# A broadcast maximum, the normaliser inside the memory matrix, and half-width stationary operands in the tail blocks of an attention and gated-MLP kernel

## The chip, the cores and the metric

The kernel runs on one core of one Trainium2 chip. The metric is the device time of one execution in microseconds (us); smaller is better. The engines are named as in the profile: PE (TensorE matmuls), PEld (its loads of stationary operands), DVE (VectorE), ACT (ScalarE), POOL (GpSimd) and SP (SyncE, which issues most DMAs).

## The reference

Attention over four batches of 576 rows and eight heads of width 64, with a gated read of a memory matrix, and then a gated MLP on all 2304 rows:

```python
scores = scale * np.matmul(q, k.transpose(0, 1, 3, 2))
scores = np.where(causal, -1000000000.0, scores)
scores = scores - scores.max(-1, keepdims=True)
a = np.exp(scores)
a /= a.sum(-1, keepdims=True) + 1e-09
local = np.matmul(a, v)
...
mem_ret = np.einsum('bhsd,bhde->bhse', q_p, M_prev)
mem_norm = np.einsum('bhsd,bhd->bhs', q_p, z_prev)[..., None] + 1e-06
mem_out = mem_ret / mem_norm
g = 1.0 / (1.0 + np.exp(-beta))[None, :, None, None]
return (g * mem_out + (1 - g) * local).astype(np.float32)
...
rms = np.sqrt(np.mean(x * x, axis=-1, keepdims=True) + 1e-06)
xn = x / rms * rms_g
g = xn @ w_gate
silu = g * (1.0 / (1.0 + np.exp(-g)))
val = xn @ w_val
return (silu * val @ w_out).astype(np.float32)
```

Here q_p is phi(q) = elu(q) + 1, and the MLP is 512 to 1536 to 512.

## The kernel before

The 2304 rows are 18 blocks of 128. Each batch has four full blocks and a rest of 64 rows; the rests of two batches share a block. These two shared blocks, 10 and 17, are called tail blocks. Blocks 0 to 3 are the first block of each batch and are computed in float32. All later blocks split each operand into a high and a low float16 part and add three products. Two blocks make a chunk of the MLP; a chunk has 12 slices F of gate and value projections (`m_proj`, tile gv) and 12 slices of the output projection (`m_down`, tile out).

The parts that matter here, with the letter under which `keep` records their instructions:

- Z, `over_partitions`: a maximum over the 128 partitions. A matmul with the column as stationary operand (L257) turns it into a row, DVE reduces the row (L259), and a second matmul (L260) spreads the result to all partitions; its reader takes it from PSUM. It is called for z, for the gain, for M of batches 0 and 1, for K and V of these batches (two columns each), for the three thirds of the gate and value weights (two columns each) and for the output weights.
- p and u, `pair_memory` and `mem32`: for blocks 0 to 3, M of a pair of heads stands in one block-diagonal tile (Mpair) and z in another (zpair). Four matmuls give the retrieved values (L786) and four give the normaliser (L790, two columns each).
- S, `u_scores` and `tail_scores`: in a tail block, the scores of one batch's rows stand in PSUM partitions 0 to 63 and those of the other in 64 to 127. Each matmul takes only half of the stationary columns (L632, L643).
- P, `u_pv` and `tail_pv`: P times V. In a tail block every head does it twice with all 128 stationary columns, once with each batch's V, into two PSUM tiles (L746 to L748); of each result only the half that belongs to that batch is read.
- M, `mem_mm`: reading the memory, in a tail block likewise twice at full width (L846).
- V, `loc_evac`: DVE scales the results out of PSUM (L877, L883).
- G is `m_proj`, D is `m_down`, U is `f64_to_f32` (a weight piece made float32 by two ACT instructions and one on DVE), E is the exponential, R turns the normalised rows of blocks 0 and 1.

The order on each engine is written out by hand: the table `ISSUE` holds a text for each engine, and `issue_in_order` reads it from left to right. `G4` takes the next four recorded instructions of kind G; `S~3` takes the one that stands fourth among those of kind S that are left. Every instruction is tied to the one before it, so each engine works strictly in that order and whatever waits holds all that stands behind it.

Of the kernel before, what the change touches and what calls it, by code (L numbers as in the profile page):

```python
# [17 lines left out]
ALU = mybir.AluOpType  # L18
AX = mybir.AxisListType
# [58 lines left out]
        "PSMPSS~3MPSS~2MPSS~1MPS2MPSMP15D6D~2G14D3S6DG9DD~2G5SGSGSGSGSGSGD2P24D3D~2GS6D4G13DD~2M8D4G4SGDD~2SGSGSGSGSG8D4"
        "G3MDD~2GMGMGMGMGMGD4GMGP25MPGPG3SGSGSGS3DD~2S3D4P9S3DD~2S4G24D4S4~2G6SGSG5P9G12S2D6G2P9G3SGSGSGSGSGSG14D6G5MGMGM"
        "GMGMP18GMGMGMG5SGSGSGSGSGSG2D6G5SGSGSGSGSGSP9G7SPGSPGSPGSPGSPGSPGPGP2D6G5MGMGMGMGMGMGMGMGP8GPG3SGSGSGSGSGSG2D6G5"  # L80
        "SGSGSGSGSGSG7P9G7D3SDSDSDGSGSGSP9GSGSG12SGSGSGSGSGSGSGSD6G5SGSGSGSGSP18GSGSGSG12D4MDMDMGMGMGP9MGMGMG12SGSGSGSGSG"
        "SGSGSD6G2P5GPGPGPSGPSGPSGPSGPSGSGSGSG5SGPSGPSGPSGPSGPSGPSGPSP5D6G9PGMPGMPGMPGMPGMPGMPGMPGMPGPGPGPGSGSGSGS5D6G9SG"
# [1457 lines left out]
```

## Time and profile before

| | |
|---|---|
| median of 3 runs | 624.98 us |
| lowest, highest | 621.99 us, 628.53 us |
| span of the profiled execution | 626.3 us |
| PE busy in it | 603.0 us, 96% |
| DVE, ACT, POOL busy | 438.0, 395.9, 134.6 us |
| first matmul | 6.0 us after the span's start |

The device time of the profiled execution is not listed apart; its span of 626.3 us lies within the three times, 1.3 us above their median. A busy share counts from an instruction's start to its modelled end, and matmuls overlap, so PE's 603.0 us are not work at its peak. What one matmul takes from its successor is read from the distance of their starts.

### The profile page before, as it was taken

The numbers are of one execution on the slowest core, as the hardware profiler recorded it, in microseconds if no ns is written. First come the engines' busy times: TensorE is split into PE (matmuls) and PEld (weight loads), VectorE is DVE, ScalarE is ACT, GpSimd is POOL, SyncE is SP. The second block draws the span as 40 slices with busy tenths as digits, with TensorE's granted clock in tenths as the row PEclk, the third lists the DMA queues.
The fourth block names the chain that finished last, engine by engine and source line by source line (L and its number), as shares of the span: only waits on it lengthen the run. The fifth ranks groups of instructions, "written<-read, shape, count | busy, mean of one in ns | idle before, by whom it ended". The sixth has DMA issues, their size and how long they took to land.

```text
span 626.3 us, 15885 instructions
## 1 busy us (share of the span) xinstructions
PE 603.0 (96%) x6124; PEld 474.2 (76%) x6124; DVE 438.0 (70%) x1287; ACT 395.9 (63%) x856; POOL 134.6 (21%) x221
## 2 busy tenths in 40 slices
PE   5979999999999999999999999999999999999996
PEld 4967887767876877888787877777788777887774
DVE  3557579989999796966777768697976756652221
ACT  4557669799789685777465656785875645523221
POOL 2040011105233222221221231122132212122111
PEclk9989999999999999999999999999999999999999
DMA  7969244588896978879388677749886544530001
GB/s 249 359 190 409 71 160 144 151 203 155 182 161 94 216 142 133 168 135 170 61 136 175 106 152 126 147 85 176 154 161 119 90 82 94 90 58 18 35 0 35
DMA packets 183787, 87.57 MB, mean 140 GB/s; under 512 B 165792, under 2 KB 165792, under 8 KB 183712
## 3 DMA queue, kind: packets, MB, share of 16 engines
q1 hardware_dynamic: 180640, 81.82, 60.9%
q10 hardware_dynamic: 3072, 4.74, 2.4%
q8 instruction: 48, 0.79, 0.6%
q14 instruction: 27, 0.22, 0.1%
HBM read 37.77 MB, written 4.72 MB: 68 GB/s over the span
## 4 chain that ended last, share of the span: by engine, by line
PE 68%; DVE 12%; DMA 7%; ACT 7%; issue 3%; SPq 1%; POOL 1%; DVEq 0%; ACTq 0%; POOLq 0%
PE gv L1108 28%; PE gv L1101 5%; PE out L1184 5%; PE out L1183 5%; PE out L1182 5%; DMA kv<-in_qkv_dram 4%; PE sc L609 3%; ACT junk L392 2%; PE tp L532 2%; DVE P L691 2%; PE sc L598 2%; DVE S L615 2%; DMA qT<-row 2%; DVE row L218 1%; PE csum L276 1%
## 5 line engine op out<-in xcount | busy, mean ns | idle before, releaser
L1108 PE MATMUL gv<-xT,wgv 128*128 128x256 f16 x2304 | 310.0, 273 | 0.5 <-DMA xT<-x 0.5
L1108 PEld LDWEIGHTS <-wgv 128*128 128x128 f16 x2304 | 220.0, 98 | 41.4 <-issue 2.4
L1147 POOL TENSOR_TENSOR h<-th,h 128x256 f16<-128x256 f32 x88 | 65.5, 744 | 282.2 <-ACT h L1146 275.3
L672 ACT ACTIVATE S<-S,nm 128x256 f32<-128x256 f32 (+3 forms) x112 | 70.7, 640 | 49.8 <-DVE nm L615 30.5
L691 DVE SCALAR_TENSOR_TENSOR P<-S,P 128x512 f16<-128x512 f32 (+2 forms) x96 | 67.7, 706 | 21.5 <-ACT P L189 21.0
L609 PE MATMUL sc<-kT,qT 128*128 128x128 f16 x576 | 79.3, 219 | 3.2 <-DVE nm L615 2.1
L1126 DVE SCALAR_TENSOR_TENSOR th<-th,gv 128x256 f32<-128x256 f32 x96 | 39.8, 415 | 60.4 <-ACT th L1125 60.1
L1125 ACT ACTIVATE th<-gv,wt 128x256 f32<-128x256 f32 x96 | 44.5, 464 | 49.4 <-PE gv L1108 46.4
L615 DVE CUSTOM_DVE_ANT_0 S<-sc,mask,qsc 128x256 f32<-128x256 f32 (+2 forms) x96 | 57.2, 610 | 18.5 <-PE sc L609 17.9
L1183 PE MATMUL out<-wo,h 128*128 128x512 f16 x176 | 66.7, 379 | 0.0
L1182 PE MATMUL out<-wo,h 128*128 128x512 f16 x176 | 66.2, 379 | 0.0
L1184 PE MATMUL out<-wo,h 128*128 128x512 f16 x176 | 66.1, 379 | 0.0
L189 ACT ACTIVATE P<-S 128x512 f16<-128x512 f32 (+2 forms) x96 | 58.0, 605 | 10.1 <-DMA PT<-P 9.3
L1146 ACT CAST h<-th 128x256 f16<-128x256 f32 x88 | 35.0, 398 | 38.4 <-DVE th L1129 34.8
L609 PEld LDWEIGHTS <-qT 128*128 128x128 f16 x576 | 48.5, 98 | 9.0 <-issue 3.1
L1101 PE MATMUL gv<-xT,wgv 128*128 128x256 f32 x192 | 46.8, 394 | 0.8 <-DVE xT L917 0.8
L1129 DVE SCALAR_TENSOR_TENSOR th<-th,wt,gv 128x256 f32<-128x256 f32 x96 | 45.7, 476 | 1.7
L1101 PEld LDWEIGHTS gv<-xT,wgv 128*128 128x128 f32 x192 | 36.5, 196 | 7.9 <-issue 1.9
L729 PE MATMUL loc<-v,PT 128*128 128x65 f16 x288 | 40.8, 193 | 1.1 <-DMA PT<-P 1.0
L731 PE MATMUL loc<-v,PT 128*128 128x65 f16 x288 | 41.0, 192 | 0.0
L730 PE MATMUL loc<-v,PT 128*128 128x64 f16 x288 | 40.5, 194 | 0.0
L1184 PEld LDWEIGHTS <-h 128*128 128x128 f16 x176 | 17.2, 98 | 19.3
(231 smaller groups left out, 1104.5 us busy)
## 6 DMA issues: line engine op xcount, KB each, us to landing
kv<-in_qkv_dram SPq DMA_DIRECT2D x40, 256.0 KB, 3.9
q<-in_qkv_dram SPq DMA_DIRECT2D x18, 256.0 KB, 3.9
wo<-in_moe_w_out_dram SPq DMA_DIRECT2D x8, 512.0 KB, 3.8
out_dram<-res ACTq DMA_DIRECT2D x16, 256.0 KB, 3.3
wgv<-in_moe_w_val_dram SPq DMA_DIRECT2D x7, 512.0 KB, 9.0
wo<-in_moe_w_gate_dram SPq DMA_DIRECT2D x7, 512.0 KB, 8.9
qT<-qT SPq DMA_DIRECT2D x28, 128.0 KB, 2.6
wgv<-in_moe_w_gate_dram SPq DMA_DIRECT2D x5, 512.0 KB, 7.5
```

The source lines that it names most:

```text
L189: got = fn(*p, **k)
L609: nc.tensor.matmul(t[:, g * w + j * P : g * w + (j + 1) * P], qT[n][:, t2, h, :], kT[blk_of[(b, j)]][:, h, :], start=(t2 == 0), stop=(t2 = ...
L615: nc.vector.tensor_tensor_reduce(out=s[:, g * w : (g + 1) * w], in0=t[:, g * w : (g + 1) * w], in1=mask[:, m0 : m0 + w], scale=qsc[n][:, 5 ...
L672: nc.scalar.activation(v_, v_, AF.Exp, bias=nm[:, g : g + 1], scale=-1.0)
L691: m = nc.vector.scalar_tensor_tensor(out=p16[:, w : 2 * w], in0=s[:, :w], scalar=PSCALE, in1=p16[:, :w], op0=ALU.mult, op1=ALU.subtract)
L1101: nc.tensor.matmul(o, wgv[:, 1 + p, o0 : o0 + P], xT[0][:, cc, at], start=(cc == 0), stop=(cc == NC - 1))
L1108: nc.tensor.matmul(o, lhs, xT[c][:, rhs, :], start=(cnt == 0), stop=(cnt == 3 * NC - 1))
L1129: nc.vector.scalar_tensor_tensor(out=th, in0=th, scalar=sc_h, in1=gvp[F][:, 1, :], op0=ALU.mult, op1=ALU.mult)
L1147: nc.gpsimd.tensor_tensor(h16[:, 1], th, h16[:, 0], ALU.subtract)
L1182: nc.tensor.matmul(o, hh, whi, start=(f == 0), stop=False)
L1183: nc.tensor.matmul(o, hh, wlo, start=False, stop=False)
L1184: nc.tensor.matmul(o, hl, whi, start=False, stop=(f == NF - 1))
```

## The change

- `over_partitions` takes the column broadcast to 128 stationary columns, so that one matmul per column puts the whole column in every partition; DVE reduces it there, and the result is in SBUF. The second matmul is gone; a call with two columns has two matmuls of the new kind.
- Mpair gets two more columns for each pair of heads, which hold z. The four small matmuls of `mem32` are gone, the other four have 130 columns instead of 128, and their results stand in two PSUM tiles. DVE then scales them with two pairs of instructions instead of one.
- `tail_pv` and the tail half of `mem_mm` take half of the stationary columns for each batch and write the two halves of one PSUM tile, the two batches in turn. The scaling in `mem_mm` and `loc_evac` then needs one instruction where it took two.
- Some small tiles are put together or moved (`few`, zz, the squares of the output weights).
- All five texts of `ISSUE` are new.

```diff
 ISSUE = {
     "PE": (
-        "T8ZZ~1T8ZT4SS~1S~2S~3Zu4T4S5S~1S~2S~3T4S4u2Tu2Th4T4u4~4T2hTh3T2u4Th8ss~3ss~2ss~1s2R8G4G4~4GG~3GZG~2G3Z~1GZT4ZT4"
...
+        "T3T~1T~1T3Z2T12SS~1S~2S~3S3T4S2S~1S~2S~3T4uS4hu3h2ThT4u~2Tu2T2h4uT4h8ss~3ss~2ss~1s~1R3R~1R~1R~1R~1RsZG3G~5G~5G~5"
...
     def over_partitions(src, n):
 
         t = ps.tile([P, 512], F32, tag="sc", name="allp")
-        nc.tensor.matmul(t[:n, :P], src, ident, start=True, stop=True)
-        v = tiny.tile([P, 1], F32, tag="vmax", name="vmax", bufs=1)
-        nc.vector.tensor_reduce(v[:n], t[:n, :P], axis=AX.X, op=ALU.max)
-        nc.tensor.matmul(t[:, P : P + n], v[:n].to_broadcast([n, P]), ident[:n, :n], start=True, stop=True)
-        return t[:, P : P + n]
+        for j in range(n):
+            nc.tensor.matmul(
+                t[:, j * P : j * P + P], src[:, j : j + 1].to_broadcast([P, P]), ident, start=True, stop=True
+            )
+        v = tiny.tile([P, 2], F32, tag="vmax", name="vmax", bufs=1)
+        nc.vector.tensor_reduce(
+            v[:, :n], t[:, : n * P].rearrange("p (j k) -> p j k", j=n), axis=AX.X, op=ALU.max
+        )
+        return v[:, :n]
...
-        for bb in range(2):
-            if hh == 0:
-                accs[n, g4, bb] = ps.tile([P, 4, D + 1], F32, tag=f"a{bb}", name=f"loc{n}_{g4}", bufs=1)
-            a = accs[n, g4, bb][:, hh, :]
-            for j in range(nb):
-                phi_, plo = pt[:, j, :], pt[:, nb + j, :]
-                vt = v16[n if j == NI else blk_of[(b + bb, j)]]
-                vhi, vlo = vt[:, h, : D + 1], vt[:, h, D + 2 :]
-                nc.tensor.matmul(a, phi_, vhi, start=(j == 0), stop=False)
-                nc.tensor.matmul(a[:, :D], phi_, vlo, start=False, stop=False)
-                nc.tensor.matmul(a, plo, vhi, start=False, stop=(j == nb - 1))
+        if hh == 0:
+            accs[n, g4] = ps.tile([P, 4, D + 1], F32, tag=f"a{g4}", name=f"loc{n}_{g4}", bufs=1)
+        a = accs[n, g4][:, hh, :]
+        for j in range(nb):
+            vt = [v16[n if j == NI else blk_of[(b + bb, j)]] for bb in range(2)]
+            for k in range(3):
+                keys = pt[:, j if k < 2 else nb + j, :]
+                for v, r in zip(vt, HALVES):
+                    src = v[:, h, D + 2 :] if k == 1 else v[:, h, : D + 1]
+                    nc.tensor.matmul(
+                        a[r, : src.shape[1]], keys[:, r], src,
+                        start=(j == 0 and k == 0), stop=(j == nb - 1 and k == 2),
+                    )
...
-        mb = sb.tile([P, 2, NC, 2, D], F32, tag="xT", name="Mpair")
-        zb = sb.tile([P, 2, NC, 2], F32, tag="h16", name="zpair", bufs=2)
+        mb = sb.tile([P, 2, NC, 2 * D + 2], F32, tag="xT", name="Mpair")
...
-            nc.gpsimd.tensor_copy(zb[r, :, :, t], z4[:, 2 * pr : 2 * pr + 2, :, t])
-        pairs[pr] = mb, zb
+            nc.gpsimd.tensor_copy(mb[r, :, :, 2 * D + t], z4[:, 2 * pr : 2 * pr + 2, :, t])
+        pairs[pr] = mb
...
-        z = ps.tile([P, H], F32, tag="sc", name="zn")
-        acc = ps.tile([P, H, D], F32, tag="a0", name=f"mem{n}", bufs=1)
+        half = [
+            ps.tile([P, 2, 2 * D + 2], F32, tag="a0", name=f"mem{n}", bufs=1),
+            ps.tile([P, 2, 2 * D + 2], F32, tag="sc", name="memz"),
+        ]
         for c in range(NC):
             nc.tensor.matmul(
-                acc[:, 2 * c : 2 * c + 2, :], q32[n][:, 1, c, :], pairs[b // 2][0][:, b % 2, c], start=True, stop=True
+                half[c // 2][:, c % 2, :], q32[n][:, 1, c, :], pairs[b // 2][:, b % 2, c], start=True, stop=True
             )
-        for c in range(NC):
-            nc.tensor.matmul(
-                z[:, 2 * c : 2 * c + 2], q32[n][:, 1, c, :], pairs[b // 2][1][:, b % 2, c], start=True, stop=True
-            )
...
+        acc = ps.tile([P, 4, D + 1], F32, tag=f"a{g4}", name=f"mem{n}_{g4}", bufs=1)
+        for hh in range(4):
+            h = 4 * g4 + hh
+            for t2 in range(2):
+                for bb, r in halves:
                     nc.tensor.matmul(
-                        acc[:, hh, :], phT[n][:, h, :], M16[b + bb][:, t2, h, : D + 1],
+                        acc[r, hh, :], phT[n][:, h, r], M16[b + bb][:, t2, h, : D + 1],
                         start=(t2 == 0), stop=(t2 == 1),
                     )
```

Line numbers differ between the two kernels. What was L746 to L748 is L763, L846 is L865, L632 and L643 are L648 and L659, L786 is L804, L257 is L271.

On PE, in the head of the program, from the float32 scores of block 1 on (sc are scores, tp transposes, mem and zn the memory read and its normaliser, loc P times V). Before:

```order
L598 MATMUL sc<-k_1_174,q_1_181 128x128 x4
L790 MATMUL zn<-zpair,q_0_157 128x2 x2
L532 MATMUL tp<-ident,S 128x128
L790 MATMUL zn<-zpair,q_0_157 128x2 x2
L532 MATMUL tp<-ident,S 128x128
L809 MATMUL loc_343<-kv_99,PT_255 128x64 x4
L532 MATMUL tp<-ident,S 128x128 x4
L790 MATMUL zn<-zpair,q_1_181 128x2 x4
```

The same place now (memz is the second of the two tiles with the retrieved values and the normaliser):

```order
L614 MATMUL sc<-k_1_168,q_1_175 128x128 x4
L831 MATMUL loc_331<-kv_96,PT_247 128x64
L804 MATMUL mem_305<-Mpair,q_0_151 128x130
L804 MATMUL memz<-Mpair,q_0_151 128x130 x2
L831 MATMUL loc_331<-kv_96,PT_247 128x64 x2
L548 MATMUL tp<-ident,S 128x128
L831 MATMUL loc_331<-kv_96,PT_247 128x64
L548 MATMUL tp<-ident,S 128x128 x4
```

The zn matmuls are gone, and the memory read of block 0, which stood ahead of block 1's scores, now stands behind them.

On PE in tail block 10, at the end of one head's scores (sct is their last part). Before:

```order
L643 MATMUL sct<-kT_4182,qT_4005 64x128
L748 LDWEIGHTS PT
L748 MATMUL loc_0_4805<-v_6_1951,PT 128x65
L747 LDWEIGHTS PT
L747 MATMUL loc_0_4821<-v_10_4295,PT 128x64
L1183 LDWEIGHTS h_4607
L1183 MATMUL out_0_3802<-wo,h_4607 128x512
L746 LDWEIGHTS PT
L746 MATMUL loc_0_4805<-v_8_3182,PT 128x65
```

The end of one head's scores in the same block now:

```order
L659 MATMUL sct<-kT_4161,qT_3984 64x128
L763 LDWEIGHTS PT
L763 MATMUL loc_0_4781<-v_0_1319,PT 64x65
L763 LDWEIGHTS PT
L763 MATMUL loc_0_4781<-v_1_1351,PT 64x65
L763 LDWEIGHTS PT
L763 MATMUL loc_0_4781<-v_0_1319,PT 64x64
L763 LDWEIGHTS PT
L763 MATMUL loc_0_4781<-v_1_1351,PT 64x64
```

All 30 half-width matmuls of an earlier head follow the 20 half-width score matmuls without anything between, where full-width matmuls of P V and of the MLP alternated. Counted over the whole order of PE, half-width matmuls stood in 16 unbroken runs of 20, and stand in 19 now, of 20 to 120.

On ACT in the head (L664 and L680 are the exponential of the scores, L1014/L1018 and L1023/L1027 the two halves of U). Before:

```order
L215 ACTIVATE zhl<-zz,zs 128x32
L1014 ACTIVATE wgv<-wgv 128x512
L1018 ACTIVATE wgv<-wgv 128x512
L664 ACTIVATE S,den<-S,nm 128x128 x4
L534 COPY q_1_181<-tp 128x512
L1014 ACTIVATE wgv<-wgv 128x512
L1018 ACTIVATE wgv<-wgv 128x512
L664 ACTIVATE S,den<-S,nm 128x128 x12
```

Now:

```order
L228 ACTIVATE zhl<-zz,few 128x32
L680 ACTIVATE S,den<-S,nm 128x128 x4
L550 COPY q_1_175<-tp 128x512
L680 ACTIVATE S,den<-S,nm 128x128 x11
L1027 ACTIVATE wgv<-wgv 128x512
L680 ACTIVATE S,den<-S,nm 128x128
L1023 ACTIVATE wgv<-wgv 128x512 x2
L1027 ACTIVATE wgv<-wgv 128x512
```

The two weight pieces that stood ahead of and between the exponentials now stand at their end.

## Rows read from the trace of the kernel before

**Rows 1.** The page: busy time by engine, granted clock in 40 slices, chain by engine.

```profile
PE 603.0 (96%) x6124; PEld 474.2 (76%) x6124; DVE 438.0 (70%) x1287; ACT 395.9 (63%) x856; POOL 134.6 (21%) x221
...
PEclk9989999999999999999999999999999999999999
...
PE 68%; DVE 12%; DMA 7%; ACT 7%; issue 3%; SPq 1%; POOL 1%; DVEq 0%; ACTq 0%; POOLq 0%
```

**Rows 2.** Windows: stretch, its length, busy us (instructions), PEclk, DMA share, GB/s.

```profile
0.00:35.00 35.00, 28.11 (x130) 25.11 (x131) 14.62 (x82) 15.74 (x51) 6.30 (x22) 1.00 0.92 308
35.00:48.00 13.00, 8.60 (x49) 7.35 (x48) 8.46 (x16) 9.16 (x20) 6.67 (x12) 0.74 0.52 164
60.00:140.00 80.00, 79.81 (x508) 62.18 (x507) 64.56 (x224) 63.06 (x149) 5.84 (x13) 1.00 0.52 154
140.00:420.00 280.00, 274.17 (x3186) 215.32 (x3185) 226.44 (x635) 200.51 (x423) 72.14 (x110) 1.00 0.76 142
300.00:352.00 52.00, 51.35 (x714) 39.98 (x713) 37.52 (x112) 30.34 (x58) 10.16 (x17) 1.00 0.68 123
520.00:562.00 42.00, 42.00 (x650) 33.71 (x649) 26.37 (x75) 18.72 (x33) 7.62 (x11) 1.00 0.47 77
```

**Rows 3.** Chain of waits, 0 to 60 us: start, us, what released the next.

```profile
0.79 0.40 SPq L387
...
11.74 0.51 PE allp L260 x2
...
15.82 2.01 PE mem L786 x8
...
24.75 0.94 PE zn L790 x4
...
26.01 0.65 PE zn L790 x4
...
29.42 1.50 PE zn L790 x8
...
54.58 0.32 PE allp L260 x2
```

**Rows 4.** The same chain, whole span.

```profile
62.32 0.89 PE mem L786 x8
...
64.08 0.79 PE zn L790 x8
...
441.87 0.89 PE sc L609 x16
...
573.08 5.24 PE gv L1108 x48
```

**Rows 5.** Timeline of PE, 318.1 to 319.2 us: start, us of one, instruction.

```profile
318.53 0.19 PE L746 MATMUL loc<-v,PT 128*128 128x65 f16 x1
...
319.17 0.19 PE L746 MATMUL loc<-v,PT 128*128 128x65 f16 x1
```

**Rows 6.** Groups of PE by form: count, busy us, mean ns, idle before.

```profile
L846 PE MATMUL mem<-M,phT 128*128 128x65 f16 x256 | 27.3, 193 | 0.6 <-DVE t L883 0.6
L747 PE MATMUL loc<-v,PT 128*128 128x64 f16 x160 | 22.9, 193 | 0.0
```

**Rows 7.** Timeline of PE, 298.2 to 299.6 us.

```profile
298.50 0.27 PE L1108 MATMUL gv<-xT,wgv 128*128 128x256 f16 x1
298.70 0.64 PE L632 MATMUL sc<-kT,qT 128*64 128x128 f16 x16
299.17 0.28 PE L643 MATMUL sct<-kT,qT 128*64 128x128 f16 x4
299.38 0.39 PE L1108 MATMUL gv<-xT,wgv 128*128 128x256 f16 x2
```

**Rows 8.** Groups of PEld by form.

```profile
L746 PEld LDWEIGHTS <-PT 128*128 128x128 f16 x160 | 15.0, 97 | 0.6
...
L632 PEld LDWEIGHTS <-qT 128*64 128x64 f16 x256 | 7.6, 109 | 2.8 <-issue 2.0
```

More of the change, by code (lines that the diff above doesn't have):

```diff
@@ L78 @@
[L78 to L82, printed above, removed]
@@ new lines @@
+        "G2G~3G~3G2G~1G3s~4s~4s~4s~4Zs5T8s~3s~3TsT3s~2G4S8sG4u2G3u2G5T4ss~1ss~3s~3ss~2ss~1s~5s~5s4s~1s~1sT4G6g2Zg2Zg6T4g5"
+        "g~1g~1g~1g~1g~1g~1g~1g~1g~1g~1g~1g~1g~1g~1g~1g~1GgGh3G2ZG3ZG2sGs~3ss~2hs2s~2s~2T4ss~1ss~1s~1s~1ss~1ss~3ss~2ss~1s"
+        "s~1s~1s~1s~1s~5s~5s~5s~5sTGT3G2gG5g4h3s4hs4g18Z2SS~1S~2S~3g2g~7g2g~5g~5g~5g~5g~5g~5g~5g~5g~5g~5g~5g~5gg~4S4g~4g~"
+        "4gTg3G4uG4u3T3ZgZg15DD~1h4Z2DTGDT3D~1G5DG2Dh3GhG7DG4DG4D9G6G~2GG~1G~1G~1G~1G20DD~1SS~7G10S~7G3DS~7GS~7S~7S~7GS4G"
+        "S~3S3G2G~6G2M~8M~8GM~8GM~8M~8M~8M~8MGM6G3SMGDGMG4SGS6G2SG6S7G6DSDG22G~2G~2G~2SG9S7ZG4PG10P5SP2SPS3P3S3P5GP7G20S5"
@@ L134 @@
+        "LFL5rXbLrklrlL2kFL3l2L2bLrkl2r2bFXrLXLr~1rkLlLlm2L2FL3bL4XrL2kr~1rbkLFrr~1rkL2XFL2rL2bLr~1LXrkL2FL2rL3Xr~1LFLrLk"
+        "L7XL3X"
     ),
@@ L772, in pair_M @@
         for t, r in ((0, slice(0, D)), (1, slice(D, 2 * D))):
-            m = nc.gpsimd.tensor_copy(pairs[b // 2][0][r, b % 2, :, t, :], m4[r, :, t, :])
+            m = nc.gpsimd.tensor_copy(pairs[b // 2][r, b % 2, :, t * D : t * D + D], m4[r, :, t, :])
             if b > 1:
@@ L865, in loc_evac @@
             return evac32(n, g4)
-        i = blocks[n][1]
-        if i < NI:
-            parts = [(slice(0, P), accs.pop((n, g4)))]
-        else:
-            parts = [(slice(bb * TR, bb * TR + TR), accs.pop((n, g4, bb))) for bb in range(2)]
+        acc = accs.pop((n, g4))
         if g4 == 0:
@@ L874, in loc_evac @@
         f = tiny.tile([P, 4], F32, tag="fm", name="fl", bufs=3)
-        for r, acc in parts:
-            tot, gain = acc[r, :, D], consts_of(n)[r, 8 + H + 4 * g4 : 12 + H + 4 * g4]
-            nc.vector.scalar_tensor_tensor(
-                out=f[r], in0=tot, scalar=1e-9 * PSCALE, in1=gain, op0=ALU.add, op1=ALU.mult
-            )
-        nc.vector.reciprocal(f, f)
-        for r, acc in parts:
-            rows = r.stop - r.start
-            nc.vector.tensor_tensor(
-                t2[r, four(n, g4), :], acc[r, :, :D],
-                f[r].unsqueeze(2).to_broadcast([rows, 4, D]), ALU.mult,
-            )
+        nc.vector.scalar_tensor_tensor(
+            out=f, in0=acc[:, :, D], scalar=1e-9 * PSCALE,
+            in1=consts_of(n)[:, 8 + H + 4 * g4 : 12 + H + 4 * g4], op0=ALU.add, op1=ALU.mult,
+        )
+        nc.vector.reciprocal(f, f)
+        nc.vector.tensor_tensor(
+            t2[:, four(n, g4), :], acc[:, :, :D], f.unsqueeze(2).to_broadcast([P, 4, D]), ALU.mult
+        )
         nc.gpsimd.tensor_tensor(
```

166 lines of the change are left out of this document (86 added, 80 removed).

## Prediction

> **What bounds the kernel now.** First the page. PE is busy for 603.0 of 626.3 us, carries 68% of the chain of waits, and no other engine is above 70% [rows 1]. A busy PE proves little by itself, so next the windows: from 60 to 140 us PE idles for 0.2 us, from 520 to 562 us not at all, and in tail block 10, from 300 to 352 us, for 0.7 us [rows 2]. DVE, the next busiest, works for 37.5 of those 52 us [rows 2]. So after the first 60 us nearly every nanosecond of PE time that goes away leaves the total, and what an edit on DVE, ACT or POOL saves does not. Two stretches are different. From 140 to 420 us PE idles for 5.8 us of 280 [rows 2]: waits for transposes and score buffers, which hang on the order of instructions. And the first 48 us run by a chain of dependent steps with PE in it most of the time.
>
> **The clock in the head.** The granted clock reads 1.00 from 0 to 35 us [rows 2], yet eight passes of the memory read took 2.01 us at 15.8 us [rows 3] and 0.89 us at 62.3 us [rows 4]: 251 against 111 ns each. I read the head as running at the lower of the two levels, 1.2 GHz, whatever the column says. From 35 to 48 us the column shows 0.74, that is 1.2 GHz for about half of the 13 us.
>
> **The change, term by term.** The sum is made against the profiled span of 626.3 us, and what it gives is then taken off the median of 624.98 us, 1.3 us below.
>
> Head, up to 35 us. The normaliser of blocks 0 and 1 goes: 0.94, 0.65 and 1.50 us on the chain [rows 3]. Two second matmuls of Z go at 0.51 us each (one stands in [rows 3], the other, at 15.31 us, is alike). That is 4.1 us at the lower clock. Its value depends on when the clock rises. If the rise stays where it is in time, PE gets 4.1 us of later work done before it, and that work would have taken half as long behind it: 2.1 us are gained. If the rise moves with the work, 4.1 us. I take 2.1, since no row ties the rise to this work. What is late next is the path from P V of block 1 through its normalisation to the first projection, and it starts earlier by the same amount; ACT's weight pieces that follow do so too, and DMAs were busy for only 0.52 of 35 to 48 us [rows 2], so the weights are there. If that path did not move, 2.1 us would be lost again. The order of SP now has K of block 0 first, ahead of q, whose issue took 0.40 us [rows 3]: -0.4 us.
>
> Normaliser of blocks 2 and 3: 0.79 us each on the chain, PE full around it (the one at 64.1 us stands for both [rows 4]): -1.6 us. The two further columns of the memory read are 2 of 130 and below 0.1 us. Two more DVE instructions for each of blocks 0 to 3 lie beside PE's work.
>
> Z behind the head: eight second matmuls, 16 passes, 0.32 us for two [rows 3], so 2.6 us go. The five calls with two columns now load 128 stationary columns twice, so 10 passes more, at the 111 ns of a float32 pass with a full load [rows 4]: 1.1 us. Net -1.5 us. The shorter trip from PE to DVE and back saves latency, which PE's other work hides; I count it at nothing, and it cannot cost.
>
> P V of the tail blocks. Three lines of 160 matmuls each, 480 in all (one line stands for the three [rows 6]). In a bare run of them 21 starts took 0.64 us, 30.5 ns each [rows 5], so they hold PE for 14.6 us. Now there are 240 pairs of half-width matmuls. No row shows such a pair with 65 moving columns, so its price is bounded. From below: two halves side by side take what one full matmul takes, 30.5 ns. From above, by the half-width scores: 16 of them, 8 pairs, take 0.47 us [rows 7], 59 ns a pair, with 128 moving columns. A full score matmul with 128 moving columns takes 56 ns [rows 4], so halving cost 3 ns a pair there. That is the nearest row, since it has the same form, and I take 30.5 + 3 = 33.5 ns: 8.0 us, -6.6 us. The bounds are -7.3 and -0.5 us.
>
> Memory of the tail blocks: 64 of 256 matmuls [rows 6], now 32 pairs at the same prices: 1.95 against 1.07 us, -0.9 us, bounds -1.0 and -0.1.
>
> Changes between full and half width. Ahead of the scores the last full matmul held PE for 0.20 us, and a matmul of that kind holds it for 0.109 us elsewhere (5.24 us for 48); behind them the next came at 299.38, 0.09 us later than two more pairs would end [rows 4, 7]. So a run costs 0.18 us, and 19 runs stand in place of 16: +0.6 us. Had P V been put in half-width runs of its own, all 16 of them would have cost 2.9 us.
>
> DVE, ACT and POOL: some 16 scaling instructions fewer on DVE in the tail blocks. Nothing on PE waits for them for long there; zero.
>
> The order otherwise. PE's coarse order is as it was; inside it matmuls of two MLP slices, or of MLP and attention, alternate more finely. The 5.8 us of waits from 140 to 420 us [rows 2] can vanish or grow; I count nothing, with 5.8 us to either side.
>
> Sum: -2.1 - 0.4 - 1.6 - 1.5 - 6.6 - 0.9 + 0.6 = **-12.5 us**: 613.8 against the profiled span, **612.5 us** against the median.
>
> **Rivals.** First, half-width pairs are no cheaper than two full matmuls: at the 59 ns of the score pairs, P V gives 0.5 us instead of 6.6 and the memory 0.1 instead of 0.9, the sum is -5.6 and the time 619.4 us. For it: loading half of the columns took 109 ns, loading all of them 97 [rows 8], so a half load is the slower one, and with 65 moving columns there is half as much time to hide it. Against it: the score pairs keep within 3 ns of a full matmul, with the loads of both halves in it. The Trainium skill has a rule for this (TensorEngine Tiling, Feature Incompatibilities): a column-tiled matmul cannot use the fast load of stationary operands; the trace agrees that the half load is slower, by 12 ns. By that rule the pair would be bound by its loads, and the time would go towards this rival's 619.4 us. The skill also states (TensorE: Matmul & The Clock Gate, Wait — 56ns, not 53.3ns?) that starts of matmuls are never less than about 25 ns apart. By that floor a pair would take 50 ns, which as an estimate puts the time near 617 us; the score halves started 29 ns apart on average, so the trace has not gone below it and leaves it open. Chance of this rival 0.17.
>
> Second, and slower than before: the loads of a pair are not hidden at all, and each pair holds PE for its load's 109 ns [rows 8]. Then P V takes 26.2 us, 11.5 more than now, and the memory 3.5, 1.5 more; with the other terms, -5.0, the time is 633 us. The place is the 272 pairs in the tail blocks. It decides from 79 ns a pair on, where 272 pairs eat the 16.6 us of full matmuls and the 5.0 us of the rest. Against it: pairs of the same width follow each other at 59 ns [rows 7], which unhidden loads of 109 ns would not allow. Chance 0.06.
>
> Third, the order. If it closes the waits of 140 to 420 us: 606.7 us, 0.12. If it doubles them, since finer alternation lets two slices end together and their buffers come free together: 618.3 us, 0.10. The finer order speaks for both, and the trace of before cannot tell.
>
> **How the numbers follow.** Forecast 0.55, with its own bounds of 608 to 617 from the head (2.1 to 4.1 us, or nothing), the pairs and the clock's low stretch of 35 to 48 us, which costs some 3 us and may come or go. Rivals: 0.17, 0.06, 0.12, 0.10. The range that leaves out no more than 2 in 10 runs from 605 to 620 us: it takes in the first rival and the order's two ends, and leaves out the slower one. About 1%, 6 us, is what a measurement of this kernel can tell from no change (its runs lie between 622 and 628.5 us). Faster by over 1%, below 618.7 us, are the forecast, the good order, and half of the first rival and of the bad order: 0.80. Within 1%: 0.14. Slower: 0.06.
>
> **What would show it.** Starts of the half-width P V some 17 ns apart on average (right), 25 to 30 (first rival) or 55 (second). The stretch of tail block 10, from the first half-width score to the last P V, shorter by some 3 us. The first float32 projection 2 to 4 us earlier than before, and no zn. PE idle between 140 and 420 us of about 6 us. The forecast fails if pairs take over 50 ns, if a stall of PE in the new order brings the lower clock with it, or if the head's path does not move.

## The result and the profile after

| | before | changed |
|---|---|---|
| first comparison, median (lowest to highest) | 626.56 us (621.99 to 628.53), 4 runs | 602.53 us (602.39 to 608.18), 4 runs |
| ratio, 95% interval | | 0.9667 (0.9583 to 0.9751) |
| repeated on another chip | 621.22 us (618.46 to 630.61), 11 runs | 603.27 us (602.32 to 608.44), 6 runs |
| ratio, 95% interval | | 0.9741 (0.9699 to 0.9783) |

The change gains 18 to 24 us, where 12.5 were forecast; 602.5 us lies below the range of 605 to 620. The runs of either kernel fall into two groups: before, eight of eleven lie between 618.5 and 622.4 us and three between 629.6 and 630.6; changed, four of six between 602.3 and 603.3 and two at 608.1 and 608.4. The second ratio leaves those three runs of before out. What divides the groups is the first thing that the experiments show.

The page of the changed kernel, its first line and the engines' shares of the chain, to be read against [rows 1]:

```profile
PE 579.4 (96%) x6082; PEld 454.3 (76%) x6082; DVE 427.4 (71%) x1278; ACT 395.6 (66%) x856; POOL 130.5 (22%) x219
...
PE 69%; DMA 15%; DVE 7%; ACT 6%; issue 2%; SPq 1%; POOL 0%; ACTq 0%; DVEq 0%; POOLq 0%
```

PE's share is as it was, and its busy time fell by 23.6 us of the 25.8 by which this profiled execution is shorter (span 600.5 us). Windows, in the columns of [rows 2]:

```profile
0.00:35.00 35.00, 26.84 (x163) 23.57 (x164) 20.77 (x97) 24.23 (x69) 9.46 (x24) 0.90 0.92 311
35.00:48.00 13.00, 11.86 (x81) 9.95 (x80) 9.75 (x28) 10.75 (x23) 2.10 (x7) 1.00 1.00 327
...
24.00:28.00 4.00, 2.15 (x16) 2.02 (x16) 1.40 (x5) 2.33 (x6) 3.41 (x7) 0.72 1.05 348
28.00:32.00 4.00, 3.63 (x16) 2.99 (x16) 2.19 (x7) 3.94 (x9) 0.32 (x1) 0.50 1.00 373
...
140.00:420.00 280.00, 276.24 (x3282) 216.60 (x3280) 221.98 (x635) 201.02 (x424) 68.36 (x111) 1.00 0.78 147
300.00:352.00 52.00, 51.64 (x710) 40.23 (x709) 36.35 (x108) 34.37 (x73) 11.84 (x27) 1.00 0.86 158
```

In the first 35 us PE now runs 163 instructions instead of 130, from 35 to 48 us 81 instead of 49. From 140 to 420 us it idles for 3.8 us instead of 5.8. PE's timeline of the head:

```profile
11.30 1.85 PE L614 MATMUL sc<-k,q 64*128 64x128 f32 x14
...
23.26 1.10 PE L831 MATMUL loc<-kv,PT 128*128 128x64 f32 x8 [0.57 <-DVE t L847]
26.21 0.93 PE L293 MATMUL csum<-kv 128*128 128x128 bf16 x7 [1.84 <-POOL xs L911]
26.94 4.08 PE L925 MATMUL xtp<-diag,t 128*128 128x128 f32 x16
...
32.03 1.35 PE L1110 MATMUL gv<-xT,wgv 128*128 128x256 f32 x4
```

The 14 passes of the scores from 11.30 us on take 132 ns on average: passes of 213 ns end at 12.1 us and passes of 111 ns follow. (The 251 ns of [rows 3] are busy time over passes; from start to start those passes took 213 ns too.) In the profile of before that turn came at 34.4 us, between the mem passes at 33.4 us; eight loc passes took 1.81 us ahead of it and 1.00 behind:

```profile
26.76 1.81 PE L809 MATMUL loc<-kv,PT 128*128 128x64 f32 x8
...
33.38 1.53 PE L786 MATMUL mem<-Mpair,q 128*128 128x128 f32 x8
...
34.85 1.00 PE L809 MATMUL loc<-kv,PT 128*128 128x64 f32 x8
```

In the changed kernel, behind the pause of 1.84 us the granted clock falls to 0.50 (the window from 28 us), and the 16 passes of xtp take 4.08 us. The first float32 projection starts at 32.03 us; before, at 44.83.

The tail block, three heads' P V behind a score run; [rows 5] had 30.5 ns for each full matmul, of which one pair replaces two. And its loads, against [rows 8]:

```profile
325.95 0.22 PE L625 MATMUL sc<-kT,qT 128*128 128x128 f16 x1
326.10 1.62 PE L763 MATMUL loc<-v,PT 128*64 128x65 f16 x90
327.65 0.39 PE L1191 MATMUL out<-wo,h 128*128 128x512 f16 x1
```

```profile
L763 PEld LDWEIGHTS <-PT 128*64 128x64 f16 x480 | 8.8, 111 | 0.6 <-issue 0.6
```

From the first half to the next full matmul 90 halves take 1.55 us: 17.2 ns each, 34.4 ns a pair with the change back to full width in it. The forecast had 33.5. Most unbroken runs are shorter, 30 halves, and share that change among fewer: counted in the same way over all 480 halves of P V a pair takes 36.5 ns.

### The profile page after: what moved, and what is told of

It reads as the page before. It is cut to its first block, busy times and chain, and to the rows that moved or that the text cites. A ratio compares the mean times of both kernels' runs of the same rounds, so it can differ in the third digit from the quotient of the medians.

```text
span 600.5 us, 15733 instructions
## 1 busy us (share of the span) xinstructions
PE 579.4 (96%) x6082; PEld 454.3 (76%) x6082; DVE 427.4 (71%) x1278; ACT 395.6 (66%) x856; POOL 130.5 (22%) x219
## 3 DMA queue, kind: packets, MB, share of 16 engines
HBM read 37.77 MB, written 4.72 MB: 71 GB/s over the span
## 4 chain that ended last, share of the span: by engine, by line
PE 69%; DMA 15%; DVE 7%; ACT 6%; issue 2%; SPq 1%; POOL 0%; ACTq 0%; DVEq 0%; POOLq 0%
PE gv L1117 31%; PE out L1191 6%; PE out L1192 6%; PE out L1193 6%; DMA PT<-P 5%; PE gv L1110 4%; PE sc L625 4%; PE csum L293 2%; DMA kv<-in_qkv_dram 2%; DMA wgv<-in_moe_w_val_dram 2%; ACT junk L408 1%; PE sc L648 1%; PE loc L763 1%; DMA wgv<-in_moe_w_gate_dram 1%; PE loc L745 1%
## 5 line engine op out<-in xcount | busy, mean ns | idle before, releaser
L1117 PE MATMUL gv<-xT,wgv 128*128 128x256 f16 x2304 | 328.5, 273 | 2.0 <-DVE th L1138 2.0
L1117 PEld LDWEIGHTS <-wgv 128*128 128x128 f16 x2304 | 213.9, 98 | 47.2 <-issue 1.7
L625 PE MATMUL sc<-kT,qT 128*128 128x128 f16 x576 | 85.2, 219 | 0.8 <-DVE nm L631 0.4
L202 ACT ACTIVATE P<-S 128x512 f16<-128x512 f32 (+2 forms) x96 | 57.8, 605 | 12.8 <-DMA PT<-P 11.7
L1191 PE MATMUL out<-wo,h 128*128 128x512 f16 x176 | 65.7, 379 | 0.2 <-ACT res L1168 0.2
L1192 PE MATMUL out<-wo,h 128*128 128x512 f16 x176 | 65.6, 379 | 0.0
L1193 PE MATMUL out<-wo,h 128*128 128x512 f16 x176 | 65.6, 379 | 0.1
L1155 ACT CAST h<-th 128x256 f16<-128x256 f32 x88 | 34.8, 398 | 36.5 <-DVE th L1138 34.4
L625 PEld LDWEIGHTS <-qT 128*128 128x128 f16 x576 | 50.6, 98 | 9.9 <-issue 1.0
L745 PE MATMUL loc<-v,PT 128*128 128x65 f16 x288 | 46.0, 193 | 3.4 <-DMA PT<-P 2.4
L747 PE MATMUL loc<-v,PT 128*128 128x65 f16 x288 | 46.2, 193 | 0.0
L746 PE MATMUL loc<-v,PT 128*128 128x64 f16 x288 | 45.3, 193 | 0.0
L1110 PEld LDWEIGHTS gv<-xT,wgv 128*128 128x128 f32 x192 | 34.9, 192 | 7.1 <-issue 1.9
L896 POOL TENSOR_TENSOR t<-t,t 128x256 f32<-128x256 f32 x28 | 21.3, 764 | 64.2 <-DVE t L893 60.1
```

What stands on the lines that cost most here:

```text
L202: got = fn(*p, **k)
L625: nc.tensor.matmul(t[:, g * w + j * P : g * w + (j + 1) * P], qT[n][:, t2, h, :], kT[blk_of[(b, j)]][:, h, :], start=(t2 == 0), stop=(t2 = ...
L745: nc.tensor.matmul(a, phi_, vhi, start=(j == 0), stop=False)
L1110: nc.tensor.matmul(o, wgv[:, 1 + p, o0 : o0 + P], xT[0][:, cc, at], start=(cc == 0), stop=(cc == NC - 1))
L1117: nc.tensor.matmul(o, lhs, xT[c][:, rhs, :], start=(cnt == 0), stop=(cnt == 3 * NC - 1))
L1191: nc.tensor.matmul(o, hh, whi, start=(f == 0), stop=False)
```

## The experiments

Medians are of all runs of a kernel; the kernel before had 621.56 us (25 runs) beside e1 to e4, 628.3 us (7) beside e5 to e8, 621.22 us (11) beside e9 to e11 and 620.39 us (13) beside e13. Starts of a projection are those of the trace's gv matmuls, sorted by start.

### The same code again: where the clock rises

e8_before is the kernel before and e9_after the changed kernel, neither edited:

```diff
 (no line changed)
```

> The kernel before once more. Theory (the code sets the rise): passes of 213 ns or more up to 33 to 35 us, first float32 projection near 45 us, some 621 to 628 us. Rival (the rise wanders by itself): it lies elsewhere, and the time with it, between 616 and 631 us.

> The changed kernel once more, for its spread and its ratio on one chip. Theory wander (the same code gets its higher clock at different places of the head, 8.5 us in one run and 12.9 us in another of the same head, 12.3 and 34 us in two of the kernel before): times between 601 and 609 us with a median of 602.5 to 607, and the kernel before between 617 and 630 us beside it; ratio 0.97 to 0.98. Rival (the first pair of profiles is typical): 602.5 us, and 626 us before, ratio 0.965.

Measured: 618.61 us for the one run of e8_before, and 603.27 us for e9_after, whose profiled run took 608.44. PE's timeline of e8_before, and windows of it (columns of [rows 2]):

```profile
10.64 1.06 PE L532 MATMUL tp<-ident,kv 128*128 128x128 f32 x4
...
12.12 0.66 PE L532 MATMUL tp<-ident,q 128*128 128x128 f32 x4
...
21.37 0.95 PE L790 MATMUL zn<-zpair,q 128*128 128x2 f32 x8
...
23.12 1.38 PE L809 MATMUL loc<-kv,PT 128*128 128x64 f32 x6
24.29 0.63 PE L532 MATMUL tp<-ident,S 128*128 128x128 f32 x2
...
26.18 1.00 PE L809 MATMUL loc<-kv,PT 128*128 128x64 f32 x8
27.94 1.10 PE L809 MATMUL loc<-kv,PT 128*128 128x64 f32 x8 [0.76 <-DVE t L825]
```

```profile
20.00:22.00 2.00, 2.00 (x21) 2.00 (x20) 1.80 (x14) 2.00 (x12) 0.00 (x0) 1.00 1.02 395
22.00:24.00 2.00, 2.00 (x13) 2.00 (x14) 1.82 (x8) 1.13 (x6) 0.72 (x1) 0.56 1.11 394
```

The same four transposes take 1.06 us at 10.64 and 0.66 us at 12.12: in this run of the kernel before the clock rises at about 12.3 us, not at 34.4, and the first float32 projection starts at 36.16 us, not at 44.83. The span is 9.4 us shorter (616.9 against 626.3 us), 8.7 of them by the first projection. The changed kernel does the same the other way round: in e9_after the 14 passes of the first scores took 2.67 us, the clock rose at 27.1 us, the first projection came at 39.06 us and the span is 606.3 us, 5.8 longer.

```profile
12.24 2.67 PE L614 MATMUL sc<-k,q 64*128 64x128 f32 x14
...
27.27 1.00 PE L831 MATMUL loc<-kv,PT 128*128 128x64 f32 x8
```

So the rise wanders by itself, and each profile of before and after that was compared first had drawn one end. Like with like, by the two early rises, e8_before and after, the change is worth 616.9 - 600.5 = 16.4 us; by the lower groups of the repeated runs 18 us. What settles the place of the rise in a run stays open.

### Extra matmuls in PE's pauses

e10_warm has 17 extra matmuls (two passes each, so 34 in the trace), e11_warmgap 34 (its line of the order is the one shown; in e10_warm it has no `%17`):

```diff
+    @keep("%")
+    def warm(k):
+        t = ps.tile([P, NC, P], F32, tag="a0", name="warm", bufs=1)
+        for j in range(k):
+            nc.tensor.matmul(t[:, j % NC], ident, ident, start=True, stop=True)
...
-        "T3T~1T~1T3Z2T12SS~1S~2S~3S3T4S2S~1S~2S~3T4uS4hu3h2ThT4u~2Tu2T2h4uT4h8ss~3ss~2ss~1s~1R3R~1R~1R~1R~1RsZG3G~5G~5G~5"
+        "%14T3T~1T~1T3%3Z2T12SS~1S~2S~3S3T4S2S~1S~2S~3T4uS4hu3h2ThT4u~2Tu2T2h4uT4h8%17ss~3ss~2ss~1s~1R3R~1R~1R~1R~1RsZG3G"
```

> The changed kernel with 17 extra float32 matmuls of 128 by 128 on the identity, whose results nobody reads: 14 ahead of the first real matmul, from about 2 us on, and 3 in the pause of 0.8 us ahead of Z at 6.5 us. Theory (TensorE's clock rises when the engine has been at work without a pause, and the head loses time by waiting for that): passes of 111 ns from 5 to 9 us on, the first float32 projection 1.5 to 3 us earlier, median 2 to 4 us below the changed kernel's in the same call, and a narrower spread. Rival (the rise wanders whatever PE does ahead of it): same times and same spread as the changed kernel, or 0.5 us more.

> The same, and 17 more extra matmuls in the pause of 1.8 us at 24.3 us, ahead of block 1's transposition for the projection. Theory (the fall to 1.2 GHz at 26 us comes from that pause): the clock stays up, the 16 matmuls of xtp take 2 us instead of 4, first float32 projection 2 us earlier than without, median 2 to 3 us below that of the kernel with the first 17 alone. Rival: the fall comes anyway, or the extra matmuls hold up the real ones: no gain, or up to 1 us lost.

Measured: e10_warm 602.94 us (601.52 to 605.91), e11_warmgap 600.90 us (598.74 to 603.35), the changed kernel beside them 603.27 (602.32 to 608.44). PE of e11_warmgap:

```profile
2.20 5.61 PE L320 MATMUL warm<-ident 128*128 128x128 f32 x28 [2.20 <-POOL ident L303]
...
24.05 4.01 PE L320 MATMUL warm<-ident 128*128 128x128 f32 x34
...
28.30 2.00 PE L936 MATMUL xtp<-diag,t 128*128 128x128 f32 x16
```

In the two profiles the clock rose at 7.7 and 6.8 us, with PE at work since 2.20 us, and none of the twelve runs reaches the 608 us of the late rises. The median of e10_warm is hardly lower, since the extra matmuls hold the first real one back: it starts at 8.07 us (7.65 in e11_warmgap), in after at 4.99. With the pause at 24 us filled the fall does not come: xtp takes 2.00 us instead of 4.08 (after), and the median falls by another 2.0 us, though two of its six runs lie among those of e10_warm. The first projection came 0.8 us earlier than in e10_warm (31.46 against 32.29), not the expected 2. So the pause of 1.84 us did bring the lower clock with it, and filling it pays, though the extra matmuls run 1.7 us beyond it (to 27.9 us). The median of e11_warmgap is below those of both kernels. That the rise wanders whatever PE does ahead of it has become less likely, with no late one in twelve runs where the changed kernel had three in ten; so few runs do not exclude it.

### The halves in the tail blocks

e1_apart is the changed kernel with the two halves no longer in turn (in mem_mm the loops change in the same way):

```diff
-        for j in range(nb):
-            vt = [v16[n if j == NI else blk_of[(b + bb, j)]] for bb in range(2)]
-            for k in range(3):
-                keys = pt[:, j if k < 2 else nb + j, :]
-                for v, r in zip(vt, HALVES):
+        for bb, r in enumerate(HALVES):
+            for j in range(nb):
+                v = v16[n if j == NI else blk_of[(b + bb, j)]]
+                for k in range(3):
+                    keys = pt[:, j if k < 2 else nb + j, :]
```

> The changed kernel with its order, but in P V and memory of the tail blocks all half-width matmuls of one batch come first and then those of the other, so that two halves no longer stand side by side. Theory: a half-width matmul is cheap only beside the one of the other half (31.6 ns a pair was read from the changed kernel's trace). Apart, each takes about 30 ns, so 272 pairs cost about 29 ns more each: +8 us, 610 us. Rival: half a matmul is short by itself, whatever stands beside it: 602.5 us and starts some 16 ns apart. The head is untouched: by the theory that order and code set when the clock rises, the passes turn from 213 to 111 ns at about 13 us again and the first float32 projection comes at about 32 us; by the rival that the rise wanders from run to run it may lie elsewhere, up to 34 us, with some 10 us on the time.

Measured: 608.14 us (607.62 to 614.45), 5.6 above the changed kernel of the first comparison and 4.9 above the repeated one. In its profile the clock rose at 8.6 us. The same 90 halves:

```profile
327.36 0.22 PE L625 MATMUL sc<-kT,qT 128*128 128x128 f16 x1
327.51 2.56 PE L763 MATMUL loc<-v,PT 128*64 128x65 f16 x90
330.00 0.61 PE L1191 MATMUL out<-wo,h 128*128 128x512 f16 x2
```

2.49 us for 90, 27.7 ns each. A pair in turn takes 34.4 ns, apart 55.3: 272 pairs times 20.9 ns are 5.7 us, the whole difference. The time is lost where the halves stand: by the marks of the table below, the stretches around the two tail blocks take 2.3 and 2.8 us longer than in after, the one between them 0.8. A half saves little by itself (27.7 ns against the 30.5 of a full matmul [rows 5]); it saves by standing beside the other one. Its loads are as long (111 ns) as the first two rivals feared, and in turn they are hidden. The Trainium skill's rule that column tiling excludes the fast load (TensorEngine Tiling, Feature Incompatibilities) agrees with the slower load, and here it costs no time. The Trainium skill says (TensorE: Matmul & The Clock Gate, Wait — 56ns, not 53.3ns?) that starts never lie less than about 25 ns apart; by that a pair could not go below 50 ns. Between the two halves the trace disagrees: 17.2 ns on average over 90 starts in turn. The 27.7 ns of one half in a row do not go below it.

e2_tails is the kernel before with the new tail_pv, mem_mm and loc_evac alone. Its order is kept, with the 30 matmuls of a head together, behind a score run where one ended nearby:

```diff
-                nc.tensor.matmul(a, phi_, vhi, start=(j == 0), stop=False)
...
+                        a[r, : src.shape[1]], keys[:, r], src,
...
-        "P2GPGPGPGPGPGPGPGPGPGPGPGP2S20PD6G20M16G4D6G16P15P7~15PP~14PP~13PP~12PP~11PP~10PP~9PP~8PP~7P15~22P15~37P52G8D6"
+        "PGPGPGPGPGPGP2S20P3D6G23M16GD6G3S20G21S20P30D6G5S20P30G19S20P30D6G24S20P30D6G20M16G4D6G16P120G8D6G24D6G24D8D~1D~"
```

> The kernel before with half-width P V and memory in the tail blocks alone; its order is kept, but the 30 matmuls of a head (and the 16 of the memory) stand together, where a score run ends nearby right behind it. Theory: P V -6.6, memory -0.9, mode switches and waits +1: about -6.5 us against the kernel before, some 619 us, head as before (passes of 213 ns or more until 34 us, first float32 projection at 45 us). Rival: most of the 24 us of the whole change lies in the order of the tail blocks and not in the halves: at most -3 us. Rival on the clock: the rise wanders from run to run, then the head may be up to 10 us shorter here too.

Measured: 620.23 us against 621.56, -1.3 us, which can't be told from no change (95% interval of the ratio 0.9988 to 1.0080). The rival's bound of 3 us held; neither theory foresaw why. The halves cost what they cost in the changed kernel: the 480 of P V take 8.99 us up to the next full matmuls, there 8.77. In its window (columns of [rows 2])

```profile
140.00:420.00 280.00, 270.14 (x3154) 209.43 (x3153) 221.58 (x622) 198.25 (x419) 70.17 (x108) 1.00 0.75 142
```

PE idles for 9.9 us, where the kernel before idled for 5.8 [rows 2]. Around tail block 10 the work went away and waits for scores took its place: PE's waits from 300 to 420 us list 3.7 us for DVE's row maxima (nm) instead of 2.1, and the stretch around the block (marks of the table below) took 88.07 us instead of 86.45. Around tail block 17 the halves did pay in the old order: 95.04 us instead of 98.19, where some 3.5 were forecast. That the matmuls which the halves saved had been covering the waits in block 10 is an inference: the 30 halves of a head were also gathered in one place here, and no run gathers full-width ones.

### Z and M

e3_zed is the kernel before with the new over_partitions alone, e4_mem with the new mem32, pair_memory and pair_M alone, e5_zm with both; the order is that of before, new matmuls at the first place of the old ones (in e4_mem and e5_zm the second half of mem stands where zn stood, for block 1 beside the first half):

```diff
-        nc.tensor.matmul(t[:n, :P], src, ident, start=True, stop=True)
+        for j in range(n):
+            nc.tensor.matmul(
+                t[:, j * P : j * P + P], src[:, j : j + 1].to_broadcast([P, P]), ident, start=True, stop=True
+            )
```

```diff
-        mb = sb.tile([P, 2, NC, 2, D], F32, tag="xT", name="Mpair")
-        zb = sb.tile([P, 2, NC, 2], F32, tag="h16", name="zpair", bufs=2)
+        mb = sb.tile([P, 2, NC, 2 * D + 2], F32, tag="xT", name="Mpair")
```

> The kernel before with the broadcast maximum (Z) alone, order kept, the matmuls at the place of the first one. Theory Z (matmuls with one stationary or one moving column keep the clock low): the rise comes at about 13 us instead of 34, which gives 10 us, and with 1.5 us behind the head and 1 us in it about -12 us, 613 us. Theory order (it is the order of the first 15 us that lets the clock rise): the passes stay at 213 ns or more until about 34 us, and the time falls by 2 to 3 us, 622 to 624 us.

> The kernel before with z inside Mpair alone (no zn matmuls), order kept. Theory order and theory Z: the clock rises at about 34 us as before; 3 us fewer of narrow matmuls at the lower level in the head, half of which is given back, and 1.6 us later: -2 to -5 us, 621 to 624 us. Theory M (the two-column matmuls between 16 and 34 us hold the clock down): the rise comes before 20 us, and the time falls by 10 us or more, 612 to 615 us.

> The kernel before with both head parts, the broadcast maximum (Z) and z inside Mpair (M), in the order of before; tail blocks as before. Each alone moved the k-th projection at 203 us by -8.8 us (Z) and -4.4 us (M) in the profile. Theory narrow (matmuls with one or two columns keep the clock low or bring it down): the rise comes at about 17.5 us as with Z alone, the fall that Z alone had at 24 us, right behind zn, does not come, and the first float32 projection stands at 35 us or earlier: -13 to -16 us at 203 us, 608 to 612 us in all. Rival (the zn matmuls only cost their own time): the fall at 24 us comes again, first projection at 37 us, 613 to 616 us.

Measured: 616.39 us (-5.2), 619.13 us (-2.4) and 616.05 us. Beside the last, the kernel before drew mostly late rises (628.3 us); against the 621.2 us that lie in the middle of its other three medians it is -5.2. The rises of the three profiles lie at 17.5, 34 and 14 us; since the same code rises at 12.3 and at 34.4 us, none of them says anything of the cause, and the theories of narrow matmuls can't be judged by them. What can be read are the stretches behind the first projection: up to the 769th float16 one, e3_zed is 1.8 us, e4_mem 1.5 us and e5_zm 3.8 us shorter than e8_before. In e5_zm the first projection came at 37.77 us, and the clock fell again behind a pause of PE that ended at 23.4 us: the third expectation's theory failed in both; the fall, the first projection and the time came as its rival had them.

In e3_zed, which keeps the zn matmuls, the clock fell behind them as in e8_before, with PE at work throughout:

```profile
24.00:28.00 4.00, 4.00 (x25) 4.00 (x24) 2.06 (x10) 0.65 (x2) 1.45 (x2) 0.57 1.03 312
```

e7_oldzed is the changed kernel with the two narrow matmuls for z and the gain:

```diff
-        got = over_partitions(ga, 1)
-        nc.vector.tensor_tensor(gmax2, got, got, ALU.mult)
+        nc.vector.tensor_copy(gmax2, old_maximum(ga, 1))
+        nc.vector.tensor_tensor(gmax2, gmax2, gmax2, ALU.mult)
...
-        pow2_scales(over_partitions(zq[:, 0:1], 1), 1, zs[:, 0:1], zs[:, 1:2])
+        pow2_scales(old_maximum(zq[:, 0:1], 1), 1, zs[:, 0:1], zs[:, 1:2])
```

> The changed kernel with its order, but the maxima of z and of the gain, the two at the head's start, by the two narrow matmuls of before. Theory narrow: the clock rises later than at the 9 to 13 us of the changed kernel, at 17 us or behind, and the time is 606 to 612 us. Rival (the order of the head's start lets the clock rise): the rise stays at 9 to 13 us, and the time is 602.5 to 604.5 us.

Measured: 606.21 us (601.28 to 607.68, 4 runs); in the profiled run, the shortest, the clock rose at 11 to 12 us and the first projection came at 32.30 us, as in after. In that run the narrow matmuls did not keep the clock down; the three others (605.7 to 607.7 us) have no profile. Whether the 3 us of the median are the narrow matmuls' or the wandering rise's, four runs don't tell.

### The order

e6_oldorder has all three parts in code and the order of before (tails as in e2_tails); e13_oldhead is the changed kernel, with the instructions of its first 135 us in the order of e6_oldorder, on all engines:

```diff
-        "T3T~1T~1T3Z2T12SS~1S~2S~3S3T4S2S~1S~2S~3T4uS4hu3h2ThT4u~2Tu2T2h4uT4h8ss~3ss~2ss~1s~1R3R~1R~1R~1R~1RsZG3G~5G~5G~5"
+        "T8Z2T12SS~1S~2S~3u2T4S5S~1S~2S~3T4S4u2T2h4T6hTh3T2u4Th8ss~3ss~2ss~1s2R8G4G~4G~4G~4G~4GG~3GZG~2G3ZGT8s4T4s4S8G6u2"
```

> All three parts of the change in code, in the order of before (half-width matmuls gathered as in the tails-alone kernel). Theory: the order is worth some 7 us ahead of 140 us (the whole change gave -20.8 us at 203 us, Z and M apart -13.2) and some 5 us around the tail blocks (halves alone gave -1.3 us where the changed kernel's trace shows -6.6): 612 to 616 us, against 602.5 us. Rival: the three parts only helped each other, and the order is worth nothing: 602 to 606 us.

> The changed kernel, whose instructions of the first 135 us stand in the order of before on all engines; behind them its own order. All three parts in code with the order of before everywhere took 614.9 us, with the new order 602.5 and 603.3 us. Theory (most of what the order gives, it gives in the head): 8 us slower than the changed kernel, 610 to 612 us. Rival (the head's difference was the wandering clock, and the order pays around the tail blocks): 603 to 606 us.

Measured: 614.91 us (611.87 to 616.75) and 612.28 us (606.63 to 615.07). All the code without the order gains 6.3 us against 621.2, about the sum of e5_zm and e2_tails (5.2 + 1.3); the order gives 11.6 more (614.91 - 603.27), 9.0 of them in the head (612.28 - 603.27) and 2.6 behind it. With rises that wander, each of these is good to some 2 us: by the three profiles, all with an early rise (12.8, 11.5 and 12.1 us), the order is worth 9.7 us (span 610.2 against 600.5). Behind the first float16 projection, where the rise no longer counts, e6_oldorder takes 485.4 us, e13_oldhead 482.9 and after 483.2, which bears out the 2.6.

Where the head's share comes from shows beside the clock's early rise. ACT of e6_oldorder, then PE:

```profile
14.63 0.66 ACT L1006 ACTIVATE wgv<-wgv 128x512 f32<-128x512 f32 x1 [0.95 <-DMA wgv<-in_moe_w_gate_dram]
15.20 0.66 ACT L1010 ACTIVATE wgv<-wgv 128x512 int32<-128x512 uint16 x1
15.75 0.39 ACT L663 ACTIVATE S<-S,nm 128x128 f32<-128x128 f32 x1
...
17.75 0.66 ACT L1006 ACTIVATE wgv<-wgv 128x512 f32<-128x512 f32 x1
18.31 0.66 ACT L1010 ACTIVATE wgv<-wgv 128x512 int32<-128x512 uint16 x1
18.86 0.39 ACT L663 ACTIVATE S<-S,nm 128x128 f32<-128x128 f32 x1
```

```profile
16.38 1.38 PE L531 MATMUL tp<-ident,S 128*128 128x128 f32 x4
18.26 1.16 PE L597 MATMUL sc<-k,q 64*128 64x128 f32 x8 [0.50 <-DVE nm L614]
...
20.60 1.81 PE L814 MATMUL loc<-kv,PT 128*128 128x64 f32 x8
...
28.11 1.10 PE L814 MATMUL loc<-kv,PT 128*128 128x64 f32 x8 [1.26 <-DVE t L830]
```

its windows,

```profile
16.00:20.00 4.00, 3.39 (x21) 2.43 (x20) 3.44 (x22) 4.00 (x17) 0.00 (x0) 0.95 1.03 416
20.00:24.00 4.00, 3.80 (x21) 3.57 (x21) 3.86 (x21) 3.58 (x20) 0.72 (x1) 0.62 1.04 390
```

and ACT of after:

```profile
13.18 0.40 ACT L680 ACTIVATE S<-S,nm 128x128 f32<-128x128 f32 x1 [0.84 <-DVE nm L631]
...
15.24 0.40 ACT L680 ACTIVATE S<-S,nm 128x128 f32<-128x128 f32 x1
...
19.53 0.67 ACT L1027 ACTIVATE wgv<-wgv 128x512 int32<-128x512 uint16 x1
```

In the old order a weight piece (two ACT instructions of 0.66 us) stands ahead of the exponentials of block 0 and another ahead of those of block 1. The latter start at 18.86 us; in the new order, with the pieces behind them, at 15.24, with the clock up since 12 to 13 us in both. From 16 to 20 us ACT is busy all the time and PE stands idle for 0.6 us in small pieces. Its longest wait there, 0.50 us, ended with DVE's row maxima (nm); DVE itself had waited 0.96 us for ACT's first weight piece and 0.56 us for an exponential. Then PE's clock falls: eight loc passes take 1.81 us at 20.60 us, where 1.00 is usual. The last P V of block 1 starts 4.9 us later than in after (28.11 against 23.26 us), the first projection 4.4 us (36.42 against 32.03). In e13_oldhead the granted clock stays at 0.50 from 20 to 28 us,

```profile
20.00:24.00 4.00, 4.00 (x20) 3.99 (x20) 3.02 (x18) 3.48 (x19) 0.18 (x1) 0.50 1.05 379
24.00:28.00 4.00, 4.00 (x20) 3.67 (x19) 2.01 (x8) 0.14 (x1) 1.27 (x2) 0.50 1.02 288
```

and the first projection comes at 39.44 us.

The kernel before has the same order of ACT. From 16 to 20 us in the first profile of before, then in e8_before:

```profile
16.00:20.00 4.00, 4.00 (x19) 3.67 (x21) 1.24 (x9) 2.61 (x11) 0.71 (x1) 1.00 1.02 415
16.00:20.00 4.00, 4.00 (x37) 3.56 (x37) 3.37 (x23) 4.00 (x18) 0.23 (x1) 1.00 1.02 416
```

With the clock up, in e8_before, ACT is as full as in e6_oldorder, but PE still has the matmuls of Z and zn and does not idle. Its last P V of block 1 starts at 27.94 us and its first projection at 36.16, no later than in e6_oldorder: in the old order, taking those matmuls out of the head gave nothing up to there. No run moved the weight pieces alone, so that it is their place by which the new order of the head gains is read from the traces and not shown.

## Why the prediction was right and wrong, step by step

By starts in the trace, e8_before against after (both with the early rise):

| stretch | forecast | measured |
|---|---|---|
| to the first float32 projection (36.16, 32.03 us) | -2.5 | -4.1 |
| to the first float16 projection (128.31, 117.29) | part of -3.1 | -6.9 |
| to the 769th of these, ahead of tail block 10 (292.83, 283.34) | rest of -3.1 | +1.5 |
| to the 1153rd, behind it (378.60, 363.74) | about -3.5 | -5.4 |
| to the 1825th, ahead of tail block 17 (518.75, 503.84) | 0 | 0.0 |
| to the end (616.9, 600.5) | about -3.5 | -1.5 |
| sum | -12.5 | -16.4 |

**Right.** The price of a pair, 33.5 ns forecast and 34.4 measured in the run of 90 halves (36.5 over all of P V); e1_apart shows that the gain in the tail blocks rests on the halves in turn. Both first rivals fall with it, and so does the 25 ns floor between the two halves. That PE's time is the total's time behind the head held for the whole change, though not around tail block 10 in e2_tails. The Z and zn terms behind the head held: -3.1 forecast, -3.8 in e5_zm. (The -6.9 and +1.5 of the second and third stretch belong together, since the order moves work over the mark between them: -5.4.)

**Right in part by luck: the sum of the tails.** -6.9 were forecast and the two stretches around them gave -6.9, but -5.4 and -1.5 instead of some -3.5 each, and the order has a hand in both: the same code in the old order, e6_oldorder, gave 0.0 and -3.1 against e8_before. (The forecast's +0.6 for three more runs of half width is 0.5 by its own 0.18 us a run, which changes nothing.)

**Failed: "The order otherwise ... I count nothing".** The order is worth 11.6 us by the medians and 9.7 by the profiles, most of it in the head. The third rival had the right sign and for the most part the wrong place: it looked for the gain in the waits from 140 to 420 us, which shrank by 2.0 us (5.8 to 3.8). The head was not looked at in that step, though the rows of ACT's order stood there: the pieces of U behind the exponentials. In the profile of before PE went through the head at 1.2 GHz and was the later one: from 16 to 20 us it was busy for 4.0 us, ACT for 2.6. With the clock up and the matmuls of Z and zn gone, PE comes up with ACT and DVE (e6_oldorder), and the order decides.

**Failed: the head's term of -2.1.** The normaliser and the second matmuls of Z were to give it by themselves. No run shows that: in the old order the first projection came at 36.42 us without them and at 36.16 with them, both with an early rise. The -4.1 came with the order. The SP term of -0.4 has its sign: the first matmul starts at 4.99 us instead of 5.96 (5.34 in e9_after). And one of the forecast's own signs of failure did come, the stall that brings the lower clock (1.84 us); it cost some 2 us (e11_warmgap against e10_warm), and the rest outweighed it.

**Failed: taking the terms apart.** The tails' -6.9 us came only together with the new order; by the old one they gave 1.3, a gain of 3.2 around tail block 17 and a loss of 1.6 to waits around tail block 10. The terms of Z and zn (-5.2 us) came to -5.2 in the old order, but not term by term: -3.8 behind the head instead of -3.1, and the rest lies within the 2 us that the rises leave open.

**Failed: the head's clock as a property of the kernel.** "If the rise stays where it is in time" took one profiled run for the place of the rise. It wanders between 12 and 34 us in the kernel before and between 9 and 27 us in the head of the changed one, which moves a run by 6 to 9 us. The first comparison's 24 us hold some 5 of that: its median of before, 626.56, stands against 620.4 to 621.6 us in three of the four later comparisons. The sum was also made against a late rise: in the runs listed the device time lies 1.7 to 2.1 us above the span, so the profile of 626.3 us belongs to a run of some 628 us and not to the median.

## What to carry to other kernels

A term that removes PE work can lose its gain to waits where the order does not let the next work come up; try the code and the order apart before trusting either. Halves of the stationary columns pay in turn, not apart. Where the clock's rise wanders, compare like stretches behind it and not whole runs. A chain at the start of a kernel should be read from more than one profile, and at both levels of the clock: the engine that has slack at 1.2 GHz may be the bound at 2.4; and a pause of PE there can be worth filling with matmuls that nobody reads.
